# Attention and mixture of experts: both heads of a pair in one product, and a lead of 16 tiles

## Chip, cores, metric

The kernel runs on one core of one Trainium2 chip. The metric is the device time of one execution in microseconds (us); the time given is the median of several runs.

## What is computed

There are 8 batches with 8 heads, 576 positions and a head size of 64, so 4608 tokens of 512 values. The attention has no softmax. A root-mean-square norm per head follows, and then a mixture of 8 experts, each with a hidden layer of 1024, where every token goes to the one expert with the highest logit.

```python
kv = einsum('bhsd,bhse->bhde', k, v)
out = einsum('bhsd,bhde->bhse', q, kv)
x = out / sqrt(mean(out * out, -1) + 1e-6) * g_norm      # then (4608, 512)
logits = x @ w_gate
e = argmax(logits)
y = (relu(x @ w1[e]) @ w2[e]) * softmax(logits)[e] * sigmoid(x @ w_output_gate)[e]
```

All of it is float32. The products of the experts run on split operands: a rounded high part and a low part, three matmuls for one product.

## The kernel before

**First part, the attention.** The loop over batches in `p1_main` adds up k-transposed times v of a batch in five steps (`kv_step`), copies the sums of the four head pairs to a tile `aug` (128 partitions: head 0 of a pair on the first 64, head 1 on the others), transposes them (`kvT_part`) and multiplies them with the gate weights (`m_part`). So `aug` holds, per head, 64 columns of k-v and 16 columns of gate logits: W = 80 columns. Between these steps the output tiles of the batch before are made, 36 tiles of 128 tokens in all. `out_tile` does the products: for each of four pairs, and for each of the two heads on its own 64 partitions, the transposed q is the weight and 80 columns of `aug` stream. The two heads write to different PSUM banks. Tiles 4, 13, 22 and 31 cross a batch and are made in two pieces of 64 rows. A float32 matmul shows as two instructions with a weight load each, so a tile has 16 matmuls, or 32. `out_rows` copies the result out on ScalarE (rows, squares, gate part), and `sums` adds up the squares on VectorE.

**Routing.** `route` works on a group of tiles (`GR`), as a generator with eight pieces: the norm's factor and its copy into the rows; the scaled gate part; its sum and the expert with the highest logit; the matmuls that number the tokens within an expert; the exponentials; the slots and the write of the finished rows to the table `xs` in HBM; position tiles `la` and `rrc`; and the matmuls with them, whose sum `tsum` gives the list of tokens of each expert. `STEPS` says after which output tile which group moves on by a piece; `TAIL` is the order written out by hand for what follows the last output tile. A digit in it moves a group on, L is a piece of the lead run, S splits a chunk of the lead's w2, Q empties what is pending of the output tiles, G gathers the lead's rows, W loads w2, and C is a block of matmuls on constants.

**The lead run.** The expert that has most tokens after the first LEAD_TILES tiles starts early, with LEAD rows (run 0) from these tiles; the rest of its rows are run 1, then come the other seven. `lead_run` splits the chunks of w1 into high and low parts (`split`, engines by `SPLITS`), transposes the gathered rows (`stage`) and makes the hidden rows (`mm1`, eight blocks). `mm2` is the second layer; the transposes of the next run's rows are put into it at fixed places. The rows of run 1 are gathered when the last group's list is known (`rows_of_lead`, line 900 on) and its rows are in `xs`.

**Queues.** All loads and the writes of rows go through SP's queue in program order: the inputs as slots come free, and the rows of the lead's tiles when the loads are out. Gathers go through GpSimd's queue. The order on TensorE, ScalarE, VectorE and GpSimd is the program's in the first part.

Of the kernel before, what the change touches and what calls it, by code (L numbers as in the profile page):

```python
# [11 lines left out]
F32 = mybir.dt.float32  # L12
# [5 lines left out]
ALU = mybir.AluOpType  # L18
# [27 lines left out]

GR = (12, 12, 12)
GROUPS = [list(range(sum(GR[:i]), sum(GR[:i+1]))) for i in range(len(GR))]
GMAX = max(GR)

LEAD_TILES = 24
LEAD_GROUP = [sum(GR[:i + 1]) for i in range(len(GR))].index(LEAD_TILES)
# [18 lines left out]

STEPS = [{14: 1, 15: 1, 17: 1, 19: 1, 20: 1, 21: 1, 23: 1, 26: 1},
         {26: 1, 27: 1, 28: 1, 31: 1, 32: 1, 33: 1, 34: 1}, {}]

HOOKS = {}
TAIL = "1GQW2C22C22CLCLLL2L2LSL2LSLSLSLLL"

COLD = (24, (8, 8, 10, 5), 5, 4, 12, 8)

GPSIMD_GROUPS = 0  # L80
APART = (2,)


SPLITS = ['VV', 'AV', 'AV', 'AV', 'AV', 'AV', 'AV', 'AV']
NORMS = "PPP"
# [52 lines left out]
def body(ctx: ExitStack, tc: tile.TileContext, kvm, rem, qT, wg, gn, w1, w2, kc, xs, tab, out):  # L138
# [305 lines left out]
    for i in range(3):  # L444
        a = c1.tile([P, NP, W], F32, name=f"aug{i}")
        augs.append(a)

    ohbs = []
# [38 lines left out]
    def kv_step(b, s):  # L487
# [20 lines left out]
        if s == 4:  # L508
            nc.scalar.copy(augs[b % 3][:, :, 0:D], ps[:, 0:NP * D].rearrange("q (p d) -> q p d", p=NP))

    def kvT_part(b):

        if b == 0:
            constant(mrp[:, 256:512], COLD[2])
        ps = kvp[:, 256:512].rearrange("q (i x) -> q i x", i=2)
        for p in range(NP):
            w = p % 2 * D
            nc.tensor.matmul(ps[w:w + D, p // 2, :], augs[b % 3][:, p, 0:D], ident, start=True, stop=True)  # L518
        t = wk.tile([P, 2, P], F32, name="kvT", bufs=1)
        nc.scalar.copy(t, ps)  # L520
        return t

    def m_part(b, kvT):
        if b == 0:
            constant(mrp[:, 256:512], COLD[3])
        for i in range(2):
            for u in range(2):
                nc.tensor.matmul(mrp[u * D:(u + 1) * D, i * 32:(i + 1) * 32], kvT[:, i, u * D:(u + 1) * D],
                                 gw[:, i, u], start=True, stop=True)
        nc.scalar.copy(augs[b % 3][:, :, D:W], mrp[:, 0:NP * 2 * E].rearrange("q (p x) -> q p x", p=NP))  # L530

# [24 lines left out]
    def out_tile(g):  # L556
# [8 lines left out]
        while n0 < (g + 1) * P:  # L565
# [3 lines left out]
            n0 = n1  # L569
        v = ps[:, :, 0:NP * W].rearrange("q u (p y) -> q u p y", p=NP)  # L570
        for p in range(NP):
            for b, r0, m in parts:
                q0 = g % 2 * P + r0

                for u in range(2):
                    r = slice(u * D, (u + 1) * D)
                    nc.tensor.matmul(v[r0:r0 + m, u, p, :], qt[g // 2][r, p, q0:q0 + m], augs[b % 3][r, p, :],  # L577
                                     start=True, stop=True)
        if g % 2:
# [3 lines left out]
    def out_rows():  # L583

        g, ps = outs.pop(0)
        gi, t, n = group_of(g)
        ss, gp, lg = gst[gi]
        c0, k, x = next(c for c in chunks if c[0] <= g < c[0] + c[1])
        xrow = x[:, g - c0]
        v = ps[:, :, 0:NP * W].rearrange("q u (p y) -> q u p y", p=NP)  # L590
        nc.scalar.copy(xrow[:, 0:DM].rearrange("q (p u d) -> q u p d", p=NP, u=2), v[:, :, :, 0:D])
        sq = wk.tile([P, H, D], F32, name="sq", bufs=4)
        nc.scalar.activation(sq.rearrange("q (u p) d -> q u p d", u=2), v[:, :, :, 0:D], AF.Square)  # L593
        nc.scalar.copy(gp[:, t].rearrange("q x (u p) -> q u p x", u=2), v[:, :, :, D:W])
        squares.append((sq, ss[:, t, :], gi if t + 1 == n else None))
# [19 lines left out]
    def route(gi):  # L615
# [23 lines left out]
        for c0, k, x in chunks_of(gi):  # L639
            nc.gpsimd.tensor_copy(x[:, :, C_RMS:C_RMS + H].rearrange("q t (p u) -> q t u p", u=2),  # L640
                                  rv[:, c0 - g0:c0 - g0 + k].rearrange("q t (u p) -> q t u p", u=2))
        yield
# [84 lines left out]
        if gi == LEAD_GROUP:  # L727
            wload(0, 1, 0)
            wload(0, 1, 1)
        yield  # L730
        las = []
        for t in range(n):
            la = wk.tile([P, P], BF16, name="la", bufs=GMAX)
            las.append(la)
            vec.tensor_scalar(out=la, in0=ni, scalar1=lon[:, t:t + 1], scalar2=None, op0=ALU.is_equal)  # L735
        shp = [P, n, E * TMAX]
# [16 lines left out]

    mark = c1.tile([P, 1], F32, name="mark")
    xwrites = []
    behind = []

    opened = [False, False]

    def after_rows(d):  # L760

        if behind:
            tc.add_manual_dep(d.ins, behind[0].ins.name,
                              mybir.DependencyInfo(mybir.DependencyClass.Sync, mybir.DependencyReason.DATA),
                              reason="order of the transfers")

    def xwrite(g, o, i):
        late = g >= LEAD_TILES
        if not opened[late]:
            xwrites.append((g, o, i))  # L770
            return
        d = nc.sync.dma_start(out=o, in_=i)
        if late:
            after_rows(d)
        if id(i) in held:
# [21 lines left out]
    def run_out(limit):  # L797
        nonlocal done_tiles
        if done_tiles < limit:
# [4 lines left out]
            if len(squares) > 1:  # L804
                sums()
            steps(done_tiles)
            load()
            if not loads and not opened[0]:
                open_rows(0)
            for step in HOOKS.get(done_tiles, ""):  # L810
                act(step)

    def act(step):
# [10 lines left out]
        elif step == "G":  # L824
# [3 lines left out]
            scale_rows(0)  # L828
            behind.append(nc.gpsimd.memset(mark, 0.0))
            for c in range(2, 4):  # L830
                after_rows(wload(0, 1, c))
            open_rows(1)
        elif step == "C":
# [326 lines left out]
```

## Time and profile before

| | |
|---|---|
| median of 3 runs | 579.88 us (579.63 to 579.93) |
| the profiled execution | 580.83 us |
| its span, first to last instruction | 579.0 us |
| TensorE busy | 549.4 us (95%) |
| VectorE busy | 256.4 us (44%) |
| ScalarE busy | 219.2 us (38%) |
| GpSimd busy | 141.4 us (24%) |
| mean granted clock of TensorE | 0.983 |

The profiled execution is timed by itself, and its span lies within that time. Busy shares are averages over the whole span, so the stretches have to be read one by one: the attention lies in the first 87 us, the routing's end and the lead run up to 152, the experts behind. In the rows below, PE is TensorE's matmuls, PEld its weight loads, DVE is VectorE, ACT is ScalarE, POOL is GpSimd and SP the queue of SyncE. L with a number is a line of the kernel.

### The profile page before, as it was taken

The numbers are of one execution on the slowest core, as the hardware profiler recorded it, in microseconds if no ns is written. First come the engines' busy times: TensorE is split into PE (matmuls) and PEld (weight loads), VectorE is DVE, ScalarE is ACT, GpSimd is POOL, SyncE is SP. The second block draws the span as 40 slices with busy tenths as digits, with TensorE's granted clock in tenths as the row PEclk, the third lists the DMA queues.
The fourth block names the chain that finished last, engine by engine and source line by source line (L and its number), as shares of the span: only waits on it lengthen the run. The fifth ranks groups of instructions, "written<-read, shape, count | busy, mean of one in ns | idle before, by whom it ended". The sixth has DMA issues, their size and how long they took to land.

```text
span 579.0 us, 10628 instructions
## 1 busy us (share of the span) xinstructions
PE 549.4 (95%) x4268; PEld 486.2 (84%) x4268; DVE 256.4 (44%) x545; ACT 219.2 (38%) x401; POOL 141.4 (24%) x158
## 2 busy tenths in 40 slices
PE   8899993689999999999999999999999999999995
PEld 6798882587898998799889987998799889879974
DVE  2138799884145554144522451344145325524410
ACT  1468681431244343223423332343244424433410
POOL 2000011307515404600352035104600631020011
PEclk9999996889999999999999999999999999999999
DMA  8999988664636422342434234423532443100000
GB/s 269 374 417 416 415 319 303 230 263 138 223 128 206 143 74 97 111 157 74 127 128 140 96 104 147 148 75 112 154 119 74 130 157 125 56 36 20 1 36 29
DMA packets 28740, 92.25 MB, mean 159 GB/s; under 512 B 4082, under 2 KB 4210, under 8 KB 28689
## 3 DMA queue, kind: packets, MB, share of 16 engines
q1 hardware_dynamic: 21952, 71.63, 34.5%
q0 software_dynamic: 6304, 19.70, 10.4%
q8 instruction: 35, 0.57, 0.4%
q10 hardware_dynamic: 432, 0.21, 0.2%
q14 instruction: 17, 0.13, 0.1%
HBM read 72.34 MB, written 19.70 MB: 159 GB/s over the span
## 4 chain that ended last, share of the span: by engine, by line
PE 82%; DVE 8%; DMA 5%; issue 2%; POOL 1%; ACT 1%; POOLq 0%; ACTq 0%; DVEq 0%
PE hps L323 35%; PE yps L372 33%; PE ops L577 4%; DMA ld<-kvm 3%; PE yps L366 3%; PE tps L285 3%; PE kvp L502 3%; DVE ss L603 1%; DMA gcol<-gn 1%; DVE la L735 1%; DVE gp L648 1%; DVE lg L652 1%; POOL xg L245 1%; DMA out<-y,oidx 0%; PE kvp L518 0%
## 5 line engine op out<-in xcount | busy, mean ns | idle before, releaser
L372 PE MATMUL yps<-whi,hT 128*128 128x512 f32 (+3 forms) x592 | 195.5, 398 | 0.5 <-ACT whi L227 0.5
L323 PE MATMUL hps<-xT,whi 128*128 128x256 f32 (+8 forms) x1024 | 190.1, 303 | 2.9 <-ACT xT L290 2.8
L323 PEld LDWEIGHTS hps<-xT,whi 128*128 128x128 f32 x1024 | 158.7, 189 | 4.1 <-ACT xT L290 3.0
L372 PEld LDWEIGHTS yps<-whi,hT 128*128 128x128 f32 (+3 forms) x592 | 110.0, 186 | 25.5 <-ACT whi L227 0.8
L323 PE MATMUL hps<-xT,wlo 128*128 128x304 f32 (+8 forms) x512 | 118.8, 303 | 0.0
L372 PE MATMUL yps<-wlo,hT 128*128 128x512 f32 (+3 forms) x296 | 116.2, 393 | 0.0
L339 DVE SCALAR_TENSOR_TENSOR hT<-hps,hT 128x512 fp32r<-128x512 f32 (+6 forms) x112 | 58.1, 519 | 125.4 <-ACT hT L338 115.4
L383 POOL DMA_INDIRECT out<-y,oidx x42 | 46.8, 1115 | 248.9 <-ACT y L382 227.0
L338 ACT ACTIVATE hT<-hps 128x512 fp32r<-128x512 f32 (+6 forms) x112 | 51.5, 460 | 146.0 <-PE hps L323 107.4
L323 PEld LDWEIGHTS hps<-xT,wlo 128*128 128x128 f32 x512 | 86.4, 189 | 0.0
L372 PEld LDWEIGHTS yps<-wlo,hT 128*128 128x128 f32 (+3 forms) x296 | 55.1, 186 | 11.4
L223 DVE SCALAR_TENSOR_TENSOR wlo<-wraw,gcol,whi 128x1024 fp32r<-128x1024 f32 x32 | 44.4, 1389 | 39.0 <-ACT whi L220 39.0
L245 POOL DMA_INDIRECT xg<-xs,gidx x42 | 42.5, 1012 | 64.9 <-ACT hT L338 23.6
L261 POOL TENSOR_TENSOR xg<-xg 128x512 f32<-128x512 f32 (+8 forms) x42 | 44.3, 1056 | 48.9 <-DMA xg<-xs,gidx 39.2
L382 ACT ACTIVATE y<-yps,tl 128x512 f32<-128x512 f32 (+3 forms) x37 | 25.4, 688 | 71.3 <-PE yps L372 70.5
L290 ACT CAST xT<-tps 128x512 fp32r<-128x512 f32 (+9 forms) x45 | 23.1, 518 | 73.3 <-PE tps L285 68.0
L291 DVE TENSOR_TENSOR xT<-tps,xT 128x512 fp32r<-128x512 f32 (+9 forms) x45 | 27.2, 605 | 49.5 <-ACT xT L290 46.9
L230 DVE TENSOR_TENSOR wlo<-wraw,whi 128x1024 fp32r<-128x1024 f32 x32 | 39.2, 1224 | 14.3 <-ACT whi L227 13.5
L577 PE MATMUL ops<-aug,ld 64*128 64x80 f32 (+1 forms) x640 | 39.5, 271 | 0.3 <-issue 0.2
L577 PEld LDWEIGHTS ops<-aug,ld 64*128 64x128 f32 (+1 forms) x640 | 33.9, 176 | 3.9 <-issue 1.6
L603 DVE TENSOR_REDUCE ss<-sq 128x8 f32<-128x512 f32 x36 | 23.7, 680 | 29.6 <-ACT sq L593 29.6
L220 ACT ACTIVATE whi<-wraw,gcol 128x1024 fp32r<-128x1024 f32 x31 | 35.5, 1145 | 0.0
(157 smaller groups left out, 386.1 us busy)
## 6 DMA issues: line engine op xcount, KB each, us to landing
wraw<-w SPq DMA_DIRECT2D x64, 512.0 KB, 3.3
ld<-kvm SPq DMA_DIRECT2D x32, 512.0 KB, 10.0
ld<-qT SPq DMA_DIRECT2D x18, 512.0 KB, 9.9
xs<-xrow SPq DMA_DIRECT2D x9, 528.0 KB, 8.7
xs<-xrow SPq DMA_DIRECT2D x2, 1320.0 KB, 11.5
xs<-xrow SPq DMA_DIRECT2D x1, 2112.0 KB
ld<-rem SPq DMA_DIRECT2D x3, 512.0 KB
xg<-xs,gidx POOLq DMA_INDIRECT x42
```

The source lines that it names most:

```text
L220: he.activation(hi, r, AF.Copy, scale=gcol[:, 0:1])
L223: eng.scalar_tensor_tensor(out=lo, in0=r, scalar=gcol[:, 0:1], in1=hi.bitcast(F32), op0=ALU.mult, op1=ALU.subtract)
L230: eng.tensor_tensor(out=lo, in0=r, in1=hi.bitcast(F32), op=ALU.subtract)
L245: gathered = nc.gpsimd.indirect_dma_start(out=x[:M, :], out_offset=None, in_=rows, in_offset=bass.IndirectOffsetOnAxis(ap=gidx[:M, p, t:t ...
L261: eng.tensor_tensor(out=v, in0=v, in1=f, op=ALU.mult)
L323: nc.tensor.matmul(ps[:, j, :n], w[:, o:o + P], x[d][:, j * N:j * N + n], start=(d == 0 and k == 0), stop=(d == 3 and k == 2))
L338: nc.scalar.activation(hh, x, AF.Relu)
L339: nc.vector.scalar_tensor_tensor(out=v(h[:, l:l + n]), in0=x, scalar=0.0, in1=hh.bitcast(F32), op0=ALU.max, op1=ALU.subtract)
L372: nc.tensor.matmul(ps[:M], a, b, start=(f == 0 and k == 0), stop=(f == 7 and k == 2))
L383: i_ = nc.gpsimd.indirect_dma_start(out=out, out_offset=bass.IndirectOffsetOnAxis(ap=oidx[:M, p, t:t + 1], axis=0), in_=y[:M], in_offset=N ...
L577: nc.tensor.matmul(v[r0:r0 + m, u, p, :], qt[g // 2][r, p, q0:q0 + m], augs[b % 3][r, p, :], start=True, stop=True)
L603: nc.vector.tensor_reduce(out=o, in_=sq, axis=AX.X, op=ALU.add)
```

## The change

Both heads of a pair go through one matmul over all 128 partitions: `aug` becomes two blocks of 80 columns, with head 0's rows in the first block, head 1's in the second and zeros elsewhere, so 160 columns stream. For that the k-v sums are first copied to a tile `kvc`, from which GpSimd fills the two blocks of `aug`; `aug` is zeroed at the start. The two heads of a pair now stand next to each other in PSUM, so the copies behind read another order. Routing works in four groups of 8, 8, 10 and 10 tiles instead of three of 12; the lead's rows come from the first 16 tiles instead of 24, so run 0 has 256 rows instead of 384 and run 1 has 436 instead of 308. The chunks of w1 for the lead are loaded, and the later rows are let through, as soon as the lead's expert is known and the inputs are out; the order of these transfers behind the lead's gather falls away. Three of ten position tiles of the last group are made on GpSimd, the pending output tiles are emptied once after tile 27, the first weight chunk's high part moves from VectorE to ScalarE, the tile of squares has three buffers instead of four, and `TAIL` is another order.

```diff
-GR = (12, 12, 12)
+GR = (8, 8, 10, 10)
-LEAD_TILES = 24
+LEAD_TILES = 16
-STEPS = [{14: 1, 15: 1, 17: 1, 19: 1, 20: 1, 21: 1, 23: 1, 26: 1},
-         {26: 1, 27: 1, 28: 1, 31: 1, 32: 1, 33: 1, 34: 1}, {}]
+STEPS = [{10: 1, 11: 1, 12: 1, 14: 1, 15: 1, 16: 1, 17: 1, 18: 1},
+         {18: 1, 19: 1, 20: 1, 22: 1, 23: 1, 24: 1, 25: 1, 26: 1},
+         {27: 1, 28: 1, 29: 1, 33: 1, 34: 1, 35: 1}, {}]
+FLUSH = (27,)
+PLACES = ['V', 'V', 'V', 'VVP']
-TAIL = "1GQW2C22C22CLCLLL2L2LSL2LSLSLSLLL"
+TAIL = "GWQCCCC2C2L33LL3L3L3LS3LS3L3LSLSLLL"
-APART = (2,)
+APART = (3,)
-SPLITS = ['VV', 'AV', 'AV', 'AV', 'AV', 'AV', 'AV', 'AV']
+SPLITS = ['AV', 'AV', 'AV', 'AV', 'AV', 'AV', 'AV', 'AV']
...
-        a = c1.tile([P, NP, W], F32, name=f"aug{i}")
+        a = c1.tile([P, NP, 2, W], F32, name=f"aug{i}")
+        nc.gpsimd.memset(a, 0.0)
...
-            nc.scalar.copy(augs[b % 3][:, :, 0:D], ps[:, 0:NP * D].rearrange("q (p d) -> q p d", p=NP))
+            kvc = kvcs[b] = wk.tile([P, NP, D], F32, name="kvc", bufs=1)
+            nc.scalar.copy(kvc, ps[:, 0:NP * D].rearrange("q (p d) -> q p d", p=NP))
+            for u in range(2):
+                r = slice(u * D, (u + 1) * D)
+                nc.gpsimd.tensor_copy(augs[b % 3][r, :, u, 0:D], kvc[r])
...
-            nc.tensor.matmul(ps[w:w + D, p // 2, :], augs[b % 3][:, p, 0:D], ident, start=True, stop=True)
+            nc.tensor.matmul(ps[w:w + D, p // 2, :], kvcs[b][:, p], ident, start=True, stop=True)
...
-        nc.scalar.copy(augs[b % 3][:, :, D:W], mrp[:, 0:NP * 2 * E].rearrange("q (p x) -> q p x", p=NP))
+        for u in range(2):
+            r = slice(u * D, (u + 1) * D)
+            nc.scalar.copy(augs[b % 3][r, :, u, D:W], mrp[r, 0:NP * 2 * E].rearrange("q (p x) -> q p x", p=NP))
...
         for p in range(NP):
+            o = ps[:, p // 2, p % 2 * 2 * W:(p % 2 + 1) * 2 * W]
             for b, r0, m in parts:
                 q0 = g % 2 * P + r0
-
-                for u in range(2):
-                    r = slice(u * D, (u + 1) * D)
-                    nc.tensor.matmul(v[r0:r0 + m, u, p, :], qt[g // 2][r, p, q0:q0 + m], augs[b % 3][r, p, :],
-                                     start=True, stop=True)
+                nc.tensor.matmul(o[r0:r0 + m], qt[g // 2][:, p, q0:q0 + m],
+                                 augs[b % 3][:, p].rearrange("q u y -> q (u y)"), start=True, stop=True)
...
-        sq = wk.tile([P, H, D], F32, name="sq", bufs=4)
+        sq = wk.tile([P, H, D], F32, name="sq", bufs=3)
...
         if gi == LEAD_GROUP:
-            wload(0, 1, 0)
-            wload(0, 1, 1)
+            lead_known.append(gi)
...
-            vec.tensor_scalar(out=la, in0=ni, scalar1=lon[:, t:t + 1], scalar2=None, op0=ALU.is_equal)
+            eng = nc.gpsimd if PLACES[gi][t % len(PLACES[gi])] == "P" else vec
+            eng.tensor_scalar(out=la, in0=ni, scalar1=lon[:, t:t + 1], scalar2=None, op0=ALU.is_equal)
...
-        if late:
-            after_rows(d)
...
+            if done_tiles in FLUSH:
+                act("Q")
             steps(done_tiles)
             load()
             if not loads and not opened[0]:
                 open_rows(0)
+            if lead_known and opened[0] and not opened[1]:
+                for c in range(4):
+                    wload(0, 1, c)
+                open_rows(1)
...
             gather(0)
             scale_rows(0)
-            behind.append(nc.gpsimd.memset(mark, 0.0))
-            for c in range(2, 4):
-                after_rows(wload(0, 1, c))
-            open_rows(1)
```

## Rows read from the trace of the kernel before

**Rows 1.** Windows: us busy of each engine, then TensorE's granted clock, DMA share, GB/s

```profile
core 0: us, PE busy (x) PEld busy (x) DVE busy (x) ACT busy (x) POOL busy (x), PEclk, DMA share, GB/s
...
28.20:87.20 59.00, 58.15 (x1193) 51.92 (x1193) 41.78 (x121) 44.56 (x115) 2.92 (x9) 1.00 0.98 390
87.20:118.30 31.10, 14.56 (x96) 11.81 (x97) 28.68 (x90) 8.79 (x19) 8.41 (x10) 0.78 0.81 280
118.30:152.70 34.40, 32.99 (x169) 29.15 (x169) 16.75 (x43) 9.59 (x15) 16.58 (x17) 0.95 0.51 168
```

**Rows 2.** The chain that ended last: start us, us, what

```profile
28.89 0.71 PE ops L577 x32
...
139.60 5.57 PE yps L372 x24
...
152.67 13.48 PE hps L323 x96
```

**Rows 3.** Timeline of TensorE's matmuls: start us, us to the last end, what

```profile
70.56 0.68 PE L744 MATMUL mrp<-rrc,la 128*128 128x96 bf16 x12
71.17 0.66 PE L518 MATMUL kvp<-ident,aug 128*64 128x128 f32 x8
71.76 1.12 PE L577 MATMUL ops<-aug,ld 64*128 64x80 f32 x16
72.81 0.43 PE L528 MATMUL mrp<-gw,kvT 128*64 128x32 f32 x8
...
81.72 5.40 PE L577 MATMUL ops<-aug,ld 64*64 64x80 f32 x96
...
105.92 1.48 PE L285 MATMUL tps<-ident,xg 128*128 128x128 f32 x12
...
136.41 0.66 PE L285 MATMUL tps<-ident,xg 128*128 128x128 f32 x4 [1.40 <-POOL xg L261]
```

**Rows 4.** Timeline of the weight loads within the tile of 71.76

```profile
71.87 0.86 PEld L577 LDWEIGHTS ops<-aug,ld 64*128 64x128 f32 x14
```

**Rows 5.** Timeline of ScalarE, its last copy for the attention

```profile
89.00 0.55 ACT L594 COPY gp<-ops 128x128 f32<-128x128 f32 x1
```

**Rows 6.** Timeline of GpSimd

```profile
74.01 2.41 POOL L640 COPY xrow<-rv 128x16 f32<-128x16 f32 x6 [24.85 <-DVE rv L638]
...
131.76 1.01 POOL L245 DMA_INDIRECT xg<-xs,gidx  x1 [23.62 <-ACT hT L338]
...
135.30 1.05 POOL L261 TENSOR_TENSOR xg<-xg 128x512 f32<-128x512 f32 x1
```

**Rows 7.** Timeline of VectorE, from the attention's end to the last indices

```profile
87.59 2.43 DVE L735 TENSOR_SCALAR la<-ni,rlon 128x128 bf16<-128x128 f32 x12
...
91.38 1.27 DVE L603 TENSOR_REDUCE ss<-sq 128x8 f32<-128x512 f32 x2
...
95.46 0.21 DVE L624 TENSOR_SCALAR ra<-ss 128x96 f32<-128x96 f32 x1
...
105.05 0.74 DVE L222 TENSOR_SCALAR whi<-wraw,gcol 128x1024 fp32r<-128x1024 f32 x1
...
107.76 0.41 DVE L291 TENSOR_TENSOR xT<-tps,xT 128x256 fp32r<-128x256 f32 x1
...
118.17 0.55 DVE L339 SCALAR_TENSOR_TENSOR hT<-hps,hT 128x384 fp32r<-128x384 f32 x1
...
119.83 1.22 DVE L230 TENSOR_TENSOR wlo<-wraw,whi 128x1024 fp32r<-128x1024 f32 x1
...
121.44 0.25 DVE L748 TENSOR_TENSOR tsum<-mrp,tsum 128x96 f32<-128x96 f32 x1
...
130.76 0.16 DVE L902 CAST gidx<-gif 128x3 int32<-128x3 f32 x1
```

**Rows 8.** DMA issues, 112 to 128 us: count, size, median us to landing

```profile
xs<-xrow SPq DMA_DIRECT2D x2, 1320.0 KB, 11.5
```

**Rows 9.** Timeline of SP's queue: the last rows written

```profile
113.27 1.81 SPq L772 DMA_DIRECT2D xs<-xrow  x3
```

More of the change, by code (lines that the diff above doesn't have):

```diff
@@ L444, in body @@
     for i in range(3):
-        a = c1.tile([P, NP, W], F32, name=f"aug{i}")
+        a = c1.tile([P, NP, 2, W], F32, name=f"aug{i}")
+        nc.gpsimd.memset(a, 0.0)
         augs.append(a)
+    kvcs = {}
     ohbs = []
@@ L569, in out_tile @@
             n0 = n1
-        v = ps[:, :, 0:NP * W].rearrange("q u (p y) -> q u p y", p=NP)
         for p in range(NP):
+            o = ps[:, p // 2, p % 2 * 2 * W:(p % 2 + 1) * 2 * W]
             for b, r0, m in parts:
                 q0 = g % 2 * P + r0
-                for u in range(2):
-                    r = slice(u * D, (u + 1) * D)
-                    nc.tensor.matmul(v[r0:r0 + m, u, p, :], qt[g // 2][r, p, q0:q0 + m], augs[b % 3][r, p, :],
-                                     start=True, stop=True)
+                nc.tensor.matmul(o[r0:r0 + m], qt[g // 2][:, p, q0:q0 + m],
+                                 augs[b % 3][:, p].rearrange("q u y -> q (u y)"), start=True, stop=True)
         if g % 2:
@@ L589, in out_rows @@
         xrow = x[:, g - c0]
-        v = ps[:, :, 0:NP * W].rearrange("q u (p y) -> q u p y", p=NP)
-        nc.scalar.copy(xrow[:, 0:DM].rearrange("q (p u d) -> q u p d", p=NP, u=2), v[:, :, :, 0:D])
-        sq = wk.tile([P, H, D], F32, name="sq", bufs=4)
-        nc.scalar.activation(sq.rearrange("q (u p) d -> q u p d", u=2), v[:, :, :, 0:D], AF.Square)
-        nc.scalar.copy(gp[:, t].rearrange("q x (u p) -> q u p x", u=2), v[:, :, :, D:W])
+        v = ps[:, :, 0:H * W // 2].rearrange("q b (h y) -> q b h y", y=W)
+        nc.scalar.copy(xrow[:, 0:DM].rearrange("q (b h d) -> q b h d", b=2, d=D), v[:, :, :, 0:D])
+        sq = wk.tile([P, H, D], F32, name="sq", bufs=3)
+        nc.scalar.activation(sq.rearrange("q (b h) d -> q b h d", b=2), v[:, :, :, 0:D], AF.Square)
+        nc.scalar.copy(gp[:, t].rearrange("q x (b h) -> q b h x", b=2), v[:, :, :, D:W])
         squares.append((sq, ss[:, t, :], gi if t + 1 == n else None))
@@ L639, in route @@
         for c0, k, x in chunks_of(gi):
-            nc.gpsimd.tensor_copy(x[:, :, C_RMS:C_RMS + H].rearrange("q t (p u) -> q t u p", u=2),
-                                  rv[:, c0 - g0:c0 - g0 + k].rearrange("q t (u p) -> q t u p", u=2))
+            nc.gpsimd.tensor_copy(x[:, :, C_RMS:C_RMS + H], rv[:, c0 - g0:c0 - g0 + k])
         yield
@@ L752, in route @@
             scatter_rows(0, 1, 0, LT)
-    mark = c1.tile([P, 1], F32, name="mark")
     xwrites = []
-    behind = []
+    lead_known = []
     opened = [False, False]
[L760 to L765, printed above, removed]
     def xwrite(g, o, i):
@@ L771, in xwrite @@
             return
-        d = nc.sync.dma_start(out=o, in_=i)
-        if late:
-            after_rows(d)
+        nc.sync.dma_start(out=o, in_=i)
         if id(i) in held:
```

## The prediction

> **What bounds the kernel now.** I read the busy time by stretch first [rows 1]. From 28.2 to 87.2 us, the attention, TensorE is busy 58.15 of 59 us at the full clock, and the DMA engines are busy too (0.98): both limits lie close together. From 87.2 to 118.3 TensorE does 14.6 us of work in 31.1, at a granted clock of 0.78, while VectorE is busy 28.7. From 118.3 on TensorE is full again (33.0 of 34.4), and then it only works off the experts. So the end moves with two things: when the attention's last product is done (87.2), and how much time passes from there until the experts' products run without a break. The chain of waits [rows 2] runs through the attention's products before and through the experts' products behind; the first product of the first expert's other rows (run 1) starts at 152.67. The experts' work is the same before and after (the same 692 rows of expert 0, cut behind 256 instead of 384).
>
> **The product of the attention.** In the timeline of TensorE [rows 3] a tile's 16 matmuls stand from 71.76 to the next block at 72.81: 1.05 us. The two heads of a pair start together on the two halves of the rows. Its loads [rows 4] give the pace: 14 of them, seven pairs, take 0.86 us, the last one's own 0.19 included, so six steps of 112 ns. What is it that takes 112 ns? 80 columns are few; the weights are 128 columns. The transposes say what a float32 matmul over all 128 rows takes to stream: 12 of 128 columns, each with its own load, start within 1.48 less 0.27 (at 105.92), so 110 ns each, 0.86 ns a column. So 80 columns stream in 69 ns and hide behind the load, which is what a pair pays for; 160 columns stream in 137 ns, and the load hides behind them. The upper bound: products of the experts [rows 2] with 308 columns take 13.48/96 = 140 ns where 308 columns at 2.4 GHz are 128, so 12 ns more each; 137 becomes 149. The row nearest in type and load is the transpose, so I take 139. The new tile is then eight products of 139 in place of eight pairs of 112: +0.22 us.
>
> The Trainium skill's page "TensorEngine Tiling (Array Packing)", section "Theoretical Speedup", promises up to twice the speed for a contraction of 64 split over row tiles, and so speaks against joining them. The rows give only 139 against 112; by the page's factor it would be 224.
>
> A block also begins with a load that nothing hides (at most the 112 of a pair) and ends with a gap before the next mode of the array (72.81; the last two of the 16 start 0.2 before it). Before, the first load and the first stream overlap those of the partner; after, the first load stands alone ahead of eight full streams: 0.112 + 8 x 0.139 + about 0.1 = 1.32 against 1.05, +0.27 for a tile between other blocks. The change of mode stays: 16-bit products on the whole array are followed by the column halves of the next block after a like gap (12 start within 0.48 from 70.56, the next block at 71.17). Four tiles cross a batch: their 32 matmuls run on quarters of the array in 0.71 us [rows 2]; after, two halves side by side take 0.06 + 8 x 0.139 = 1.17 plus at times a gap, +0.45. From 28.2 on there are 24 tiles between other blocks, 4 in a row at the end (among the 96 matmuls from 81.72, [rows 3]) and 4 that cross: 24 x 0.27 + 4 x 0.22 + 4 x 0.45 = 9.2 us. About 0.85 us of TensorE's idle time there [rows 1] may take some of it: 8.4. A fourth routing group brings its matmuls into this stretch: one more list (12 in 0.6 us at 70.56) and one more count of the like size, for 8 tiles together 0.8. The attention ends 9.2 us later, at 96.4. Bounds: 136 gives 8.3, 149 gives 11.5. If the load still set the pace (112), 0.8.
>
> **What hides.** The block-diagonal tile is filled by GpSimd in two copies of 64 x 256: between the 0.40 us of its small copies (2.41 for six) and the 1.05 of its products of 512 [rows 6], so 0.8 to 2.1 us. Meanwhile TensorE does the transposes of k-v (0.6), another tile (1.05) and the gate product (0.4) [rows 3] ahead of the first use; beyond these the last 5 tiles would wait, at most 0.3. The zeroing at the start lies before 8 us, in the wait for the first data. ScalarE copies the gate part in two pieces, 0.2 more, hidden alike.
>
> **The transfers that move.** On SP's queue the order becomes: rows of 16 tiles (4.3 MB) after the last load, four chunks of w1 (2.1 MB), rows of the third group (2.7) in step 35, w2 (2.1), rows of the last group (2.7). Before, the last rows went out at 113.27 [rows 9], behind w1 and w2. With 9 us more of attention, slots are freed more slowly and the queue is not full: the 6.4 MB for the lead run need 16 us at 390 GB/s [rows 1], from the last load's landing at about 80 to 96. GpSimd's gather for the lead then ends about when the attention does. That hides as long as the lead's rows aren't wanted before 96.4 + 6.
>
> **The tail.** VectorE works without a break from 87.6 to the last list's total at 121.44 [rows 7], 34.2 us after the attention's end. What leaves this stretch: four of the five late sums (1.27 for two: 2.5), the lead's list (between the sums ending at 92.65 and 95.46 lie 2.8, two sums of them: 1.5, of which 0.3 stays: 1.2), the first weight half (0.75), four of six low parts of the lead's rows with their waits (six 0.41 in 3.7; two of double size 1.4: 2.3), seven of 24 position tiles (2.43/12 each: 1.4; GpSimd takes three), a tenth of the routing steps between 95.46 and 105.05 for ten tiles instead of twelve (1.0). What comes in, since the new order puts it ahead of the total: another low part each of w1 and w2 (1.2 each) and two of hidden rows (0.55 for 384 columns: 0.9 for two). The last sum now waits for ScalarE, which finished 2.3 us after TensorE [rows 5]: 1.2. So 34.2 - 9.2 + 4.5 = 29.5 us after the end of attention. The matmuls of this list end some 0.3 before the total; TensorE's last four blocks of lead products wait for them and then take 4 x 12 x 0.12 = 5.8 (256 columns at 2.4 GHz and the 12 ns). Half clock at their start costs up to 1.7 (from 118.3 to 152.7 the clock was 0.95 of 34.4 us); I take 1.2. With nine products of the second layer (5.57/24 = 0.231 each [rows 2]) TensorE asks for the next rows at 29.2 + 5.8 + 1.2 + 2.1 = 38.3.
>
> Before, the indices came 9.3 us after the total (130.76), behind the lead's VectorE work, and the gather at 131.76 [rows 6]; the transposes started 4.65 later [rows 3], 49.2 after the attention. After, less of that work stands behind the total. Lower bound: indices after 1.2 us, at 30.7. The rows themselves bound it too: written at about 23, with up to 11.5 us to land [rows 8], 31 to 34. I take 33, transposes at 37.7: TensorE and the rows come together at about 38.3. From there before: 16.3 us to run 1. After: 39 second-layer products (9.0) and four blocks of transposes (0.5 each): 11.0. And one tile more is left for run 1: 128 columns in 96 products (5.1) and 24 x 0.231 (5.5) = 10.6. Tail after: 38.3 + 11.0 + 10.6 = 59.9; before: 65.4. Gain 5.5.
>
> Sum: +9.2 - 5.5 = +3.7 us. The profiled execution took 580.83 us for a span of 579.0; the median is 579.88, 0.95 lower, which I take as the same in every stretch: 583.6.
>
> **The rivals.**
> - Forecast, 0.48: slower by 3.7. Own range 580.5 to 587, from the two product bounds and 2.5 us on the meeting point at 38.3.
> - The indices stay behind the lead's VectorE work, 0.17: gather 10.3 after the total as before, at 39.8, transposes at 44.4, nothing gained in the tail (66.0): +9.8, 589.7; less if TensorE waits partly: 587 to 590. Speaks for it: VectorE's order puts it there today. Against: fewer of the lead's steps follow.
> - The two terms cancel, 0.10: the rows at about 34.6 after the attention instead of 38.3: 579.9.
> - Faster through the tail, 0.13: the place is the meeting point; it decides below 33.4. At 32.5 the time is 577.8. It needs the list's total near 25, so VectorE caught up during the longer attention (it is busy 41.8 of 59 us there). Against: its steps hang on the last tile.
> - The load remains the product's price, 0.10: eight of 112 ns where eight pairs of 112 stood, the attention 0.8 longer, the tail 5.5 shorter: 575.2. Against it: 110 ns for 128 columns in the transposes.
> - The heads' row halves really were worth a factor of two, 0.02: 8 x 0.112 more a tile, 32 tiles: +28.7 less 5.5: 603.
>
> "TensorE: Matmul & The Clock Gate", section "LDWEIGHTS (loading the stationary operand)", of the Trainium skill prices a load by its columns alone, not its rows; by that the fifth case would hold, if the load set the pace of the new product too. The 112 ns of a pair agree with 128 columns at 1.2 GHz (107 ns).
>
> **The numbers.** A measurement of this kernel can tell about 0.2%, 1.16 us, from no change. Faster: 0.13 + 0.10 = 0.23. Same: 0.10 and 0.05 from the forecast's lower edge. Slower: 0.43 + 0.17 + 0.02 = 0.62. The range runs from 576.5 to 588: it leaves out the fifth and last cases and half of the second.
>
> **What would show it.** Eight products a tile, their starts about 139 ns apart; the attention's last product near 96 us; the last list's total some 29.5 us later; the first transposes of run 1 near 134.7; run 1's first product near 145.7, with one tile more left to do. Product starts at 112 ns or transposes of run 1 before 130 would make me wrong on the fast side, transposes after 138 on the slow side.

## Result: 8.1 us slower, and the profile after

The changed kernel takes 587.84 us (586.51 to 589.48), the kernel before took 579.75 beside it: a ratio of 1.0146, 95% interval 1.0114 to 1.0179. The forecast was 583.6, so the sign was right and the size was not: 587.84 lies outside the forecast's own range (580.5 to 587) and in the band of the second rival. A ratio here is that of the undisturbed executions and a median is over all of them, so the two need not divide out. The profiled execution of the changed kernel took 587.19 us for a span of 585.4, 6.4 more than the span of before.

The windows of after, cut where those of [rows 1] were cut (end of the attention, early in the lead, first product of run 1):

```profile
core 0: us, PE busy (x) PEld busy (x) DVE busy (x) ACT busy (x) POOL busy (x), PEclk, DMA share, GB/s
28.20:96.60 68.40, 65.63 (x915) 57.66 (x916) 52.20 (x163) 48.94 (x127) 12.32 (x26) 1.00 0.98 389
96.60:128.30 31.70, 17.14 (x141) 15.44 (x139) 28.13 (x85) 10.39 (x19) 6.25 (x6) 0.87 0.59 218
128.30:149.10 20.80, 19.05 (x105) 16.80 (x104) 12.45 (x35) 6.18 (x11) 14.29 (x15) 0.88 0.55 178
```

The ends of the sums below are the starts of single products, the attention's last and run 1's first, for the kernel before:

```profile
86.84 0.28 PE L577 MATMUL ops<-aug,ld 64*128 64x80 f32 x2
...
152.51 0.44 PE L323 MATMUL hps<-xT,whi 128*128 128x308 f32 x2
```

(The chain in [rows 2] counts run 1 from 152.67, 0.16 later.) The attention's last product starts at 96.46 instead of 86.85, run 1 at 149.10 instead of 152.51. What stands behind run 1's start grew from 426.5 to 436.3, because one more tile is left for it. So three terms decide: 9.6 us later out of the attention, 13.0 us less from there to run 1 (52.6 instead of 65.7), 9.8 more behind it; together the 6.4 of the spans.

TensorE's timeline of after, beside [rows 3]:

```profile
77.12 0.50 PE L753 MATMUL mrp<-rrc,la 128*128 128x96 bf16 x8 [0.56 <-DVE rrc L750]
77.55 0.66 PE L529 MATMUL kvp<-ident,kvc 128*64 128x128 f32 x8
78.13 1.35 PE L587 MATMUL ops<-aug,ld 128*128 128x160 f32 x8
79.42 0.42 PE L539 MATMUL mrp<-gw,kvT 128*64 128x32 f32 x8
79.67 0.66 PE L509 MATMUL kvp<-ld 128*64 128x64 f32 x16
81.43 1.32 PE L587 MATMUL ops<-aug,ld 128*128 128x160 f32 x8 [1.10 <-issue]
...
93.26 3.49 PE L587 MATMUL ops<-aug,ld 128*128 128x160 f32 x24
...
96.46 0.30 PE L587 MATMUL ops<-aug,ld 128*128 128x160 f32 x1
...
138.20 0.66 PE L290 MATMUL tps<-ident,xg 128*128 128x128 f32 x4 [1.75 <-POOL xg L266]
...
149.10 0.56 PE L328 MATMUL hps<-xT,whi 128*128 128x436 f32 x2
```

A tile between other blocks stands from 78.13 to the next block at 79.42: 1.29 us where 1.05 stood. Its products lie 136 ns apart by their starts, the first 0.24 ahead of the second; so do the 24 from 93.26, the first of them 0.21 ahead. Two waits in these rows are new: 0.56 for the list of the second group, 1.10 ahead of a product at 81.43 (the gate copies for its batch came only at 80.83, behind six copies of two earlier tiles that the extra flush had put ahead of them on ScalarE). The transposes of run 1 come at 138.20, later than the 136.41 of before, and past the 138 that the prediction named as its sign of being wrong on the slow side.

VectorE of after, from the attention's end to the index of run 1, beside [rows 7]:

```profile
95.55 0.87 DVE L723 SCALAR_TENSOR_TENSOR rlon<-rhk,slots 128x10 f32<-128x10 f32 x1
...
96.42 1.02 DVE L725 TENSOR_SCALAR rdn<-rdn 128x10 f32<-128x10 f32 x1
...
99.93 2.04 DVE L744 TENSOR_SCALAR la<-ni,rlon 128x128 bf16<-128x128 f32 x10
...
116.59 0.42 DVE L344 SCALAR_TENSOR_TENSOR hT<-hps,hT 128x256 fp32r<-128x256 f32 x1 [1.13 <-ACT hT L343]
...
128.38 0.26 DVE L757 TENSOR_TENSOR tsum<-mrp,tsum 128x96 f32<-128x96 f32 x1 [0.39 <-PE mrp L753]
...
130.33 0.16 DVE L903 CAST gidx<-gif 128x4 int32<-128x4 f32 x1
```

GpSimd and SP's queue of after, beside [rows 6] and [rows 9], the queue's last line from the view of its line of the kernel:

```profile
95.36 2.05 POOL L266 TENSOR_TENSOR xg<-xg 128x512 f32<-128x512 f32 x2 [3.92 <-DMA xg<-xs,gidx]
...
132.00 1.05 POOL L250 DMA_INDIRECT xg<-xs,gidx  x1 [6.37 <-DVE hT L344]
...
137.10 2.04 POOL L266 TENSOR_TENSOR xg<-xg 128x512 f32<-128x512 f32 x2
```

```profile
122.05 0.96 SPq L773 DMA_DIRECT2D xs<-xrow  x2
...
DMA to landing us min/median/max: 5.0/6.7/8.4
```

The gather of run 1 starts at 132.00; before it started at 131.76. Everything the tail was to give hangs on this number, and in absolute time it did not move. The last list's total comes 31.9 us behind the attention's last product (96.46), the index 1.95 behind that (130.33), and the last rows, issued from 122.05, land by 131.0. So the rows come last, and the gather starts 1.0 behind them; in e1 and e6 below it starts 0.95 and 0.97 behind their landing. Where the index comes last instead (before, e5, e7 to e10, e12, e13), the gather starts 0.6 to 0.8 behind the index copy's end.

### The profile page after: what moved, and what is told of

It reads as the page before. It is cut to its first block, busy times and chain, and to the rows that moved or that the text cites. A ratio compares the mean times of both kernels' runs of the same rounds, so it can differ in the third digit from the quotient of the medians.

```text
span 585.4 us, 10076 instructions
## 1 busy us (share of the span) xinstructions
PE 557.5 (95%) x3959; PEld 492.9 (84%) x3959; DVE 262.7 (45%) x574; ACT 223.3 (38%) x409; POOL 154.0 (26%) x179
## 4 chain that ended last, share of the span: by engine, by line
PE 83%; DMA 5%; DVE 5%; issue 3%; POOL 2%; ACT 1%; POOLq 0%; ACTq 0%; DVEq 0%
PE hps L328 35%; PE yps L377 33%; PE ops L587 5%; DMA ld<-kvm 3%; PE yps L371 3%; PE tps L290 3%; PE kvp L509 2%; DMA gcol<-gn 1%; POOL la L744 1%; DVE ss L613 1%; PE kvp L529 1%; DVE la L744 1%; POOL xg L250 1%; DMA out<-y,oidx 0%; ACT xrow L601 0%
## 5 line engine op out<-in xcount | busy, mean ns | idle before, releaser
L328 PE MATMUL hps<-xT,whi 128*128 128x256 f32 (+7 forms) x1024 | 191.7, 305 | 0.0
L328 PE MATMUL hps<-xT,wlo 128*128 128x256 f32 (+7 forms) x512 | 119.7, 305 | 0.0
L328 PEld LDWEIGHTS hps<-xT,wlo 128*128 128x128 f32 x512 | 87.7, 192 | 0.3
L295 ACT CAST xT<-tps 128x512 fp32r<-128x512 f32 (+8 forms) x42 | 22.7, 544 | 74.1 <-PE tps L290 74.1
L587 PE MATMUL ops<-aug,ld 128*128 128x160 f32 (+1 forms) x320 | 48.7, 310 | 1.6 <-issue 1.1
L296 DVE TENSOR_TENSOR xT<-tps,xT 128x512 fp32r<-128x512 f32 (+8 forms) x42 | 26.7, 637 | 45.1 <-ACT xT L295 45.1
L587 PEld LDWEIGHTS ops<-aug,ld 128*128 128x128 f32 (+1 forms) x320 | 40.2, 179 | 5.0 <-issue 3.6
L225 ACT ACTIVATE whi<-wraw,gcol 128x1024 fp32r<-128x1024 f32 x32 | 36.7, 1146 | 0.0
```

The source lines that it names most:

```text
L225: he.activation(hi, r, AF.Copy, scale=gcol[:, 0:1])
L328: nc.tensor.matmul(ps[:, j, :n], w[:, o:o + P], x[d][:, j * N:j * N + n], start=(d == 0 and k == 0), stop=(d == 3 and k == 2))
L587: nc.tensor.matmul(o[r0:r0 + m], qt[g // 2][:, p, q0:q0 + m], augs[b % 3][:, p].rearrange("q u y -> q (u y)"), start=True, stop=True)
```

## The experiments

**e1: the product as before, the new order kept.** The two heads go back to two products on row halves, all else is the changed kernel.

```diff
-                nc.tensor.matmul(o[r0:r0 + m], qt[g // 2][:, p, q0:q0 + m],
-                                 augs[b % 3][:, p].rearrange("q u y -> q (u y)"), ...)
+                for u in range(2):
+                    r = slice(u * D, (u + 1) * D)
+                    nc.tensor.matmul(v[r0:r0 + m, u, p, :], qt[g // 2][r, p, q0:q0 + m], augs[b % 3][r, p, :], ...)
```

> The new groups, lead and order behind the attention, but the attention's product as before: each head on its own half of the rows, 80 columns. Theory A, the joined product is the loss (150 ns for a product against 112 for a pair, some 9 us of attention), and the new tail gives about 2 us back: the attention's last product near 88 to 90 us, the tail as in the changed kernel (52.5 us to run 1's first product, one tile more left), the time 578 to 581. Theory B, the joined product costs nothing because the loads bound the attention, and the new groups and order are the loss: the time stays near 586 to 588.

584.28 us, ratio 1.0059 (1.0038 to 1.0081): the new groups, lead and order cost 3.4 us by themselves, between the two theories. At a like mean clock (0.977 to 0.979) e1 took 582.95 to 584.34 and the kernel before 579.58 to 582.08, so the clock alone is not it. The attention's last product starts at 91.00 instead of 86.85, the list's total comes at 124.90, the gather at 128.04, run 1 at 147.32. But part of this late end is not the new order's. The window from 25 us on of e1, and below it that of e5, a later run with the same attention:

```profile
25.00:32.30 7.30, 7.30 (x106) 6.39 (x106) 2.06 (x3) 5.00 (x13) 0.00 (x0) 0.53 1.03 420
```

```profile
25.00:32.30 7.30, 6.37 (x148) 5.72 (x150) 3.17 (x5) 5.66 (x14) 0.00 (x0) 1.00 1.03 418
```

In the profiled execution of e1 the granted clock was 0.53 there; in e5 it was 1.00, and the last product came at 87.93, 3.1 earlier. To compare attentions I therefore count from the first product of tile 4, the first tile that crosses a batch: it starts at 28.82 before and 28.93 after, at 30.44 in e1 and between 27.88 and 30.07 in the others. With 9.8 us more behind run 1, its start would have had to come 9.8 us earlier than before to break even; counted so it came 6.8 earlier.

**e2: the joined product alone, in the order of before.** To make room, two block diagonals instead of three, and three buffers of squares.

> The kernel before with the joined product alone: groups of 12, lead of 24 tiles, old order. Only two buffers of the block-diagonal tile and three of the squares, for space. Theory A: the attention ends 8 to 10 us later, near 96, and the time is 587 to 590, since the old tail stays. Theory B: the time stays near 580.

583.86 us, ratio 1.0077 (1.0053 to 1.0101): 4.5 us, again between the two theories. The two halves of the change add up within their intervals: 3.4 + 4.5 = 7.9, beside the 8.5 by the ratio of the whole. The attention's last product starts at 93.05, 6.2 us later (6.7 counted from tile 4), so some 1.5 us come back behind it: the last list's total moves by only 4.7 us (121.44 to 126.11; 5.2 from tile 4). VectorE gets more of its work done during the longer attention: from there to the total it is busy 30.5 us, before 31.9.

**e3: two products of 80 columns over all 128 rows, and e4: 96 columns for each head.** Both keep everything else of the changed kernel. e3 multiplies each pair's weights with the two halves of the block diagonal one after the other; e4 puts 16 columns of zeros between and behind, 192 columns for a pair.

```diff
+                for u in range(2):      # e3
+                    nc.tensor.matmul(o[r0:r0 + m, u * W:(u + 1) * W], qt[g // 2][:, p, q0:q0 + m], augs[b % 3][:, p, u], ...)
...
-        a = c1.tile([P, NP, 2, W], F32, name=f"aug{i}")
+        a = c1.tile([P, NP, 2, 96], F32, name=f"aug{i}")
```

> The changed kernel, but each pair's product cut in two of 80 columns over all 128 rows, so 16 matmuls a tile with a load each, on the whole array. If a load over all rows takes as long as a pair's (112 ns) and nothing shares it, the starts lie 112 to 125 ns apart, a tile takes 1.9 us and the attention about 23 us more than in the changed kernel. If only the columns count, the starts lie 69 to 85 ns apart and a tile stays near 1.3 us.

> The changed kernel with 16 columns of zeros behind each head's 80, so that 192 columns stream in a product instead of 160. If the stream sets the pace of the joined product, its starts move from 150 to about 177 ns (0.83 ns a column) and the attention ends some 7 to 8 us later. If the load or a fixed cost sets it, they stay at 150.

605.87 and 594.11 us, one execution each. A tile and the block behind it, of e3:

```profile
102.44 2.01 PE L588 MATMUL ops<-aug,ld 128*128 128x80 f32 x16
104.39 0.42 PE L539 MATMUL mrp<-gw,kvT 128*64 128x32 f32 x8
```

and of e4:

```profile
92.31 1.57 PE L587 MATMUL ops<-aug,ld 128*128 128x192 f32 x8
93.81 0.42 PE L539 MATMUL mrp<-gw,kvT 128*64 128x32 f32 x8
```

In e3 the starts are 112 ns apart although 80 columns would stream in 68: there a floor sets the pace that does not come from the columns streamed. I take it for the load of 128 columns of weights; a fixed cost of the same size would look alike, and none of these runs changed the size of the load. In e4 they are 162.5 apart, in the changed kernel 136: 26.5 ns for 32 columns, 0.83 ns each, and 136 is 0.85 a column. So the product of 160 columns is paced by its columns and the load hides, as the prediction had it. In the forms of 160 and 192 columns the first product of a tile stands alone ahead (0.24 and 0.27 us to the second; 0.17 in e3).

**e6: the changed kernel without the new waits.** No extra flush, the steps that use a list two tiles later, the third group's spread out.

```diff
-STEPS = [{..., 17: 1, 18: 1}, {..., 25: 1, 26: 1}, {27: 1, 28: 1, 29: 1, ...}, {}]
+STEPS = [{..., 17: 1, 20: 1}, {..., 25: 1, 28: 1}, {28: 1, 29: 1, 30: 1, ...}, {}]
-FLUSH = (27,)
+FLUSH = ()
```

> The changed kernel without the emptying after tile 27, the third group's first steps one tile later, and the last steps of groups 0 and 1 moved two tiles behind the step that makes their position tiles. Theory: three waits of TensorE in the attention (0.65 and 0.86 us for position tiles, 1.3 us behind the copies of the emptied tile) are owed to these; without them the attention ends about 2.3 us earlier, near 94, and the time falls by about 2 us to 585 to 586.5. Rival: VectorE's backlog takes them back in the tail, and the time stays at 587 to 588.

587.84 us, ratio 1.0111 (1.0074 to 1.0149): not to be told from the changed kernel, although the attention ended 2.8 us earlier (93.69; 2.2 counted from tile 4). VectorE of e6, and what TensorE waited for:

```profile
94.07 0.16 DVE L723 SCALAR_TENSOR_TENSOR rlon<-rhk,slots 128x10 f32<-128x10 f32 x1
...
126.60 0.26 DVE L757 TENSOR_TENSOR tsum<-mrp,tsum 128x96 f32<-128x96 f32 x1 [0.38 <-PE mrp L753]
```

```profile
PE tps L290 <- POOL xg L266: 3.0, 1, 3.0
```

The total comes 1.8 us earlier than in the changed kernel and the gather too (130.16), but from the transposes to run 1 it takes 13.7 instead of 10.9 us, at a granted clock of 0.81 from 126.6 to 150.0. So the waits were real and cost the attention 2.2 us, and removing them was worth nothing measurable in time; the last section shows that the 2.8 us more up to run 1 are the clock's.

**e5, e7 and e8: another order of the tail.** Routing steps of the last groups go ahead of the lead's products: e5 on e1, e7 on the changed kernel, e8 on e1 with the edit of e6.

```diff
-TAIL = "GWQCCCC2C2L33LL3L3L3LS3LS3L3LSLSLLL"
+TAIL = "GWQCCCCCL33LL3L33L3L2L2SL3SL3LSLSLL"
```

> The halves of the row for the product (as in the run with halves and the new order, 584.3 us) and another order of the tail: the last group's steps up to the write of its rows come ahead of the third group's list and of most weight halves. Theory: what sets run 1's start in the new order is the write of the last rows, issued 25.5 us after the attention and landed 9 us later, so their gather starts with them; then the write moves some 6 to 8 us forward, the gather is bound by the last list instead, some 3 us earlier than now, and the time falls to 580 to 582. Rival: VectorE's total work sets it, whatever its order; then the time stays within 1 us of 584.

> The changed kernel with the other order of the tail alone (last group's rows written ahead of the third group's list). Theory: as in the run with halves, the gather for run 1 starts some 3 us earlier (now 35.4 us after the attention) and the time falls by 2 to 4 us to 584 to 586. Rival: VectorE's total work sets it; 587 to 588.

> Halves of the row for the product, no emptying, the lists' last steps spread, and the other tail: everything of the change but the joined product, with its waits taken out. If the terms add up (4 for the product, 2 for the waits, 3 for the tail) it takes 577 to 580 us and is level with or faster than the kernel before. If VectorE's total work sets the tail, 581 to 583.

584.45 (ratio 1.0079, 1.0035 to 1.0122), 588.80 (1.0132, 1.0093 to 1.0170) and 585.05 (1.0076, 1.0055 to 1.0096). None gains over its base, and e8 is slower than either theory had it. In e8 the attention ends at 86.40, as early as before, and still the time is 4.4 us longer. TensorE of e8 shows two waits for gathered rows:

```profile
97.59 1.12 PE L290 MATMUL tps<-ident,xg 128*128 128x128 f32 x4 [5.59 <-POOL xg L266]
...
132.40 1.12 PE L290 MATMUL tps<-ident,xg 128*128 128x128 f32 x4 [4.52 <-POOL xg L266]
```

The lead's own rows come late: gathered from 89.39, beside the third group's rows that SP's queue writes from 88.43, they are scaled from 96.50. VectorE, which splits them in its order, idles 4.2 us for them (0.28, 2.77 and 1.17), and the last list's total comes at 123.78, 95.9 us after tile 4 (before 92.6); then TensorE waits again, 4.52 us, for the rows of run 1. So with an early end of the attention the lead's rows are the next thing in line; no run moved them alone.

**e9 and e10: routing first, so that the late rows go out early.** e9 is e8, e10 the changed kernel, both with

```diff
+TAIL = "GWQCCCCL3333CCC33LLL2L2L3L3LSLSLSLSLL"
```

> The kernel with halves, no emptying and spread lists (585.1 us), with a third order of the tail: the last group's steps up to the write of its rows come first, then the lead's rows and weights, and its position tiles and list come before the last four blocks of the lead's hidden rows. Theory: VectorE works off its queue in order, and in the new order the lead's weight halves and hidden rows stand between the last group's steps; there the last list's total came 37 us after the attention. With the steps in front it comes near 28, the gather for run 1 near 30 instead of 40, and run 1's first product some 8 to 10 us earlier: 572 to 577 us. Rival: what bounds is not the order but the transfers (the late rows' landing) or TensorE's lead work; then the time stays within 2 us of 585.

> The changed kernel with this third order of the tail alone. Theory as above: the gather for run 1 moves from 35.5 us after the attention to 28 to 31, the time falls from 587.8 to 580 to 584. Rival: within 2 us of 587.8.

588.78 (1.0135, 1.0087 to 1.0183) and 596.59 (1.0289, 1.0247 to 1.0332): e10 is slower than the changed kernel, e9 by 0.6% than e8 with intervals that just overlap; neither theory had this. The late rows land early as wanted, 23.2 us behind the attention in e10 instead of 34.6. But then the index is late. VectorE, GpSimd and TensorE of e10:

```profile
127.50 0.25 DVE L757 TENSOR_TENSOR tsum<-mrp,tsum 128x96 f32<-128x96 f32 x1
...
135.97 0.17 DVE L903 CAST gidx<-gif 128x4 int32<-128x4 f32 x1
...
136.78 1.05 POOL L250 DMA_INDIRECT xg<-xs,gidx  x1 [14.76 <-issue]
...
143.98 1.11 PE L290 MATMUL tps<-ident,xg 128*128 128x128 f32 x4 [7.96 <-POOL xg L266]
```

8.5 us lie between the total and the index, filled with low parts of weights and hidden rows of the lead on VectorE, and TensorE waits 7.96 us for the rows.

**e11, e12 and e13: the index directly behind the total.** The five instructions that make run 1's index move from behind the tail into the last list: e11 in the kernel before, e12 in e10, e13 in e9.

```diff
+        if last:
+            gl = sm.tile([P, TMAX], F32, name="gl")
+            rows_of_lead(gl)
+            vec.tensor_copy(gif[:, 0, LT:], gl[:, LT:])
+            vec.tensor_copy(gidx[:, 0, LT:], gif[:, 0, LT:])
```

> The kernel before, with the index of run 1 (one product, one sum, one combination and two copies on VectorE) computed directly behind the total of the last routing list instead of behind the later work of the lead. Theory, that the indices set when the rows of run 1 come: in the kernel before TensorE waits 1.40 us for these rows, the total comes at 34.6 us behind the start of the attention's last product and the gather at 44.9, but the late rows land at 40.4, so the gather can move to 41 or 42 and the time falls by up to 1.4 us, 578.5 to 579.5. Rival, that the late rows or TensorE's own work of run 0 set it: no change within 0.5 us.

> The variant of the changed kernel that lists routing first (late rows landed at 23.2 us behind the attention), with the index of run 1 computed directly behind the total of the last list. There the total came at 127.50 us, the index copy at 135.97, the gather at 136.78, and TensorE waited 7.96 us for the rows. Theory, that VectorE's queue ahead of the index copy holds the gather: gather near 129.5, TensorE's wait gone or under 1 us, time 589.5 to 591 instead of 596.6. Rival, that something else holds the gather (the landing of the rows, GpSimd's own queue): gather stays within 1 us of 136.8, time stays at 595 to 597.

> The same index edit on the variant with the product of before (two row halves), no waits of TensorE and routing listed first. There the total came at 122.48 us, the index copy at 130.85 and the gather at 131.66; the time was 588.8. Theory: gather near 124.3, rows of run 1 scaled near 130.5, time 581.5 to 583.5, and with it the smaller lead would do what was forecast for it, without beating the kernel before, since one tile more behind run 1's start costs 9.8 us. If it comes below 579.4 the new groups and the early index beat the kernel before. Rival: no change, 586 to 590.

579.34 (ratio 0.9978, 0.9957 to 0.9998), 586.74 (1.0098, 1.0073 to 1.0124) and 582.29 (1.0025, 0.9998 to 1.0051). The same rows in e12:

```profile
128.46 0.25 DVE L757 TENSOR_TENSOR tsum<-mrp,tsum 128x96 f32<-128x96 f32 x1
...
130.71 0.16 DVE L766 CAST gidx<-gif 128x4 int32<-128x4 f32 x1
...
131.64 1.61 POOL L250 DMA_INDIRECT xg<-xs,gidx  x1 [8.96 <-ACT hT L343]
...
138.68 0.66 PE L290 MATMUL tps<-ident,xg 128*128 128x128 f32 x4 [1.99 <-POOL xg L266]
```

The order of VectorE's queue held the gather: with the index 2.25 us behind the total, the gather comes 5.1 us earlier than in e10, TensorE's wait falls from 7.96 to 1.99, and the ratio falls by 1.9% with the joined product and by 1.1% with the halves. In the kernel before, the same edit brings the index from 130.76 to 123.01, but the gather only from 131.76 to 129.90 and the transposes to 134.93, and the time down by 0.2%: something else holds the gather there, neither the index nor the late rows (landed at 127.1), and no run shows what. e11 is the one version that beats both kernels, by so little that its interval ends just short of no change. e13 says what groups of 8 and 10 and a smaller lead are worth without the joined product, without the waits and with the index early: no gain over before, at most 0.5% loss. Its expectation held; e12 came out some 3 us better than its own.

## Why the prediction had the sign and not the size

**The product: right.** It took 139 ns between bounds of 136 and 149; the starts are 136 apart. A tile between other blocks grew by 0.24 us (forecast 0.27). The two rivals on the load are out: e3 shows that the floor of 112 sets the pace only for fewer columns, and no factor of two was lost. The price of a column was right by luck: it was read off transposes of 128 columns that start 110 ns apart, and e3 shows a floor of 112 ns for 80 columns with such a load, so those transposes could not tell streaming from loading. That 0.86 ns is the price of streaming is what e4 shows (0.83). The price of a load by its columns alone, in the section on LDWEIGHTS of the Trainium skill's page "TensorE: Matmul & The Clock Gate", agrees with these 112 ns (128 columns at 1.2 GHz are 107), but it is not what the joined product pays. Counted from tile 4, the joined product lengthens the attention by 6.7 us in the old order (e2) and 6.8 to 7.5 in the new (e6 against e8, the changed kernel against e1 and e5), where the forecast had 8.4. Of the difference 0.7 is the tile (0.24 for 0.27, 24 times); the rest was not taken apart.

**The attention's end: right sum, wrong parts.** Forecast 9.2 later, measured 9.6. From tile 4 to its last product the attention takes 58.0 us before, 64.8 in e2, 65.3 in e6 and 67.5 in the changed kernel (67.5 as well in e7, e10 and e12, which have the same attention). So the new order took 2.8 us (2.0 and 2.5 with the halves, e5 and e1), not the 0.8 counted for its matmuls. The larger part, 2.2, are the waits of 0.56 and 1.10 us in the rows above and their like, which e6 removes: I counted the fourth group's work and not what its earlier steps would make TensorE wait for. That the sum came out is luck: the product was 1.7 less than forecast, the new order 2.0 more.

**The tail: the step that failed.** "After, 59.9; before 65.4, gain 5.5" measured 62.4 (52.6 to run 1 and 9.8 behind it) against 65.7: 3.2, and 2.3 of the miss. One tile more in run 1 was right (9.8 for 10.6), and so was the way from transposes to run 1 (10.9 for 11.0). The meeting point was wrong: 41.7 us behind the attention instead of 38.3. The list's total came at 31.9 instead of 29.5, and the late rows were written at 26.1 instead of 23 and landed at 34.6; the gather, which waits for them, came at 35.5 instead of 33. From gather to transposes it took 6.2 instead of 4.65: the kernel issues all gathers of run 1 ahead of the first scaling, and these are now four instead of three (some 1.3 us each). Both the total and the write hang on VectorE's list, and by its rows these make it late: an instruction of 1.02 us that takes 0.17 in e6, a wait of 1.13 for ScalarE's hidden rows, 0.62 for its weights, together 2.6. No run took them out one by one.

Behind this lies an error of form. I tied VectorE's list to the end of the attention. It is not tied to it: counted from tile 4, when the attention grows by 6.7 to 7.5 us through the product, the total moves by 4.5 to 5.2 (before to e2, e1 to the changed kernel, e5 to e7), and when e6 shortens the attention by 2.2, it moves by 1.3. So neither the 9.2 of the attention nor the 5.5 of the tail is a term in the time; by the ratios of these three pairs the product is worth 3.1 to 5.0 us, and the new order 3.4 (e1). The second I explain by one identity: the smaller lead puts 9.8 us behind run 1's start and takes away only the fewer products of run 0 ahead of it, so it pays only if the gather comes well earlier in absolute time. In the changed kernel it comes at 132.00, before at 131.76. No run changed the size of the lead alone, so how the 3.4 divide between the lead, the groups and the order of the tail is open.

**The rivals.** The second, indices behind VectorE's work of the lead, was not what held the changed kernel, although the time lies in its band: the index came 1.95 us behind the total, and the rows landed 0.7 after that. It is exactly what holds e10, though, and e12 shows its price, some 10 us. The third, two terms that cancel, wanted the rows at about 34.6; the transposes came at 41.7. The fourth, faster through the tail, asked for a total at 25 us; no order of the tail brought it below 31 with the joined product.

**From the profiled executions to the medians.** The spans differ by 6.4, the medians by 8.1. The profiled execution of after lies 0.65 below its median, that of before 1.1 above the median of the runs beside it. I had taken the offset as the same for both. With it the miss of 4.4 (8.1 for 3.7) is whole: 0.4 in the attention, 2.3 in the tail, 1.7 here.

## What to carry over

A stage that ends later does not shift what follows by as much: find the engine that works through both stages (VectorE here), and move its chain, not the stage's end. When work is cut smaller so that a first part can start early, what it leaves behind must be weighed in full against the absolute time at which the second part's inputs exist; if that time does not move, the cut only costs. The few small instructions that release a large transfer belong directly behind what they read, since in a queue in order their price is everything that stands ahead of them, up to the point where something else holds the transfer (e11). And before two traces are compared by absolute times, look whether both got going equally early: a stretch at the lower clock in the first 32 us moved e1's attention by some 2 us, which is no effect of its edit.

## What the runs showed of the hardware that was not expected

The granted clock falls for a few us again in the middle of the lead, and not in each kernel's profiled execution. The windows of the changed kernel show it:

```profile
128.30:132.00 3.70, 3.70 (x19) 3.70 (x19) 3.10 (x16) 0.88 (x2) 0.00 (x1) 0.50 0.47 176
132.00:136.00 4.00, 4.00 (x30) 4.00 (x30) 2.81 (x6) 2.14 (x4) 3.17 (x3) 0.82 0.53 141
136.00:140.00 4.00, 2.25 (x14) 1.84 (x14) 3.97 (x8) 0.97 (x2) 3.71 (x4) 1.00 0.56 222
```

TensorE is busy throughout the first two windows, at 1.2 GHz in the first (0.50); it fell after a stretch, 122.0 to 126.6, in which TensorE was busy for 0.94 us. In e1 the lower clock comes behind 3 us of idle time, and in e13 it doesn't come at all:

```profile
130.00:135.00 5.00, 1.99 (x18) 1.79 (x16) 2.88 (x9) 1.25 (x3) 4.36 (x5) 0.96 0.79 270
135.00:140.00 5.00, 5.00 (x20) 4.23 (x21) 0.75 (x2) 1.00 (x2) 4.66 (x5) 0.70 0.25 70
```

```profile
121.00:131.00 10.00, 8.38 (x62) 7.65 (x60) 9.96 (x21) 5.67 (x9) 6.03 (x5) 1.00 0.42 136
131.00:142.00 11.00, 10.92 (x55) 8.84 (x56) 4.09 (x14) 2.79 (x5) 9.44 (x11) 1.00 0.51 163
```

The executions of e13 show it in part: 578.7 to 580.1 us at a mean clock of 0.979 to 0.986, 583.8 and 584.0 at 0.978, but 582.2 to 582.5 at 0.981 to 0.984; so the clock does not tell all of the spread. What it costs can be read from the stretch between the transposes and run 1, which has the same matmuls (55 or 56 in the traces), with TensorE busy throughout, in all runs of the new groups. The changed kernel, and below it e6:

```profile
138.20:149.10 10.90, 10.90 (x56) 8.85 (x56) 4.34 (x13) 2.78 (x5) 9.04 (x10) 1.00 0.51 155
```

```profile
136.39:150.08 13.69, 13.69 (x55) 11.05 (x56) 2.61 (x8) 2.78 (x5) 11.80 (x13) 0.78 0.55 153
```

In e1 it took 12.32 us at 0.88, in e12 12.50 at 0.86, in e7 13.47 at 0.80. Time times clock is 10.7 to 10.9 us in all five, so the 2.8 us between e6 and the changed kernel are the clock's. Why it fell in the one and not in the other is open: just ahead, TensorE had waited for its rows 1.75 us in the changed kernel and 3.02 in e6, but also 1.99 in e12 and 4.53 in e7.

VectorE's instructions of ten elements a row took 0.87 and 1.02 us while GpSimd scaled rows of 512 elements beside them (95.36 to 97.4), and 0.16 and 0.17 in e6, where GpSimd began only behind them. There the next five small writes were hit, 1.30 us instead of the 0.45 at 97.78 in the changed kernel. VectorE and GpSimd of e6, then of the kernel before:

```profile
94.73 1.30 DVE L734 TENSOR_TENSOR xrow<-rdn 128x2 f32<-128x2 f32 x5
...
94.75 2.21 POOL L266 TENSOR_TENSOR xg<-xg 128x512 f32<-128x512 f32 x2 [2.43 <-DMA xg<-xs,gidx]
```

```profile
104.16 0.98 DVE L700 TENSOR_SCALAR rogs<-rogs 128x12 f32<-128x12 f32 x1
...
104.07 1.04 POOL L261 TENSOR_TENSOR xg<-xg 128x512 f32<-128x512 f32 x1 [0.35 <-DMA xg<-xs,gidx]
```

No run moved only this, so it is a coincidence in time, but it goes with GpSimd's work in these three kernels and in e7. The Trainium skill's page "SBUF — State Buffer", section "SBUF: two separate sides", has these two engines take a shared pair of ports in turn, each for a whole instruction, where VectorE's instruction reads two inputs from SBUF or runs in a mode that uses two ports; 0.7 and 0.9 us of delay are within the 1.02 that one of GpSimd's two instructions takes, so the trace does not contradict it.
